# Sixteen GpSimd rectifications of an attention bias, each written as two instructions in two alternating forms

## The chip, the cores and the metric

The kernel runs on one core of a Trainium2 chip. The metric is the device time of one execution in microseconds. TensorE appears in the profile as PE (matmuls) and PEld (weight loads), VectorE as DVE, ScalarE as ACT, GpSimd as POOL and SyncE as SP. All transfers but one are issued by SP.

## The reference, cut to what matters

The input is `q`, `k`, `v` of 8 batches x 8 heads x 576 positions x 64. Attention has a bias that depends on two positions and the head; a gated two-matrix network follows it.

```
rel  = pos[:, None] - pos[None, :]
x    = log1p(|rel|) / log1p(max(pos, 1))[:, None]     # 576 x 576
h    = maximum(x[..., None] * w1 + b1, 0)             # 32 hidden units
bias = h @ w2                                         # one value per head, row, column
out  = softmax(q k^T / 8 + bias) v   -> gated network -> 8 x 576 x 512
```

## The kernel before, in words

**The bias stage.** The first 65 us of the run make the bias, 16 rows of it at a time, in 36 blocks (`bias_rows(m)`, lines 294 to 386). log1p(|rel|) has the same values in every row, so one table `gt` (128 partitions x 576) serves all rows. The 128 partitions hold 4 groups of 32 hidden units, and a *rectification* (`relu`, lines 310 to 325) takes four of the block's rows at once: it multiplies `gt` by a number per partition (`sct`, which holds w1 / log1p(row)), and takes the maximum with another number per partition (`nb1`, which is -b1). So what it stores is max(x w1, -b1) = max(x w1 + b1, 0) - b1, and the constant that is left over is added later through `cadd`. The width is `w`, the longer side of the block's rows, between 304 and 576 columns. A block has four rectifications: the first is always on ScalarE (line 316, a true relu), the other three on VectorE or GpSimd (line 318). Of these 108, 92 are on VectorE and 16 on GpSimd.

Then TensorE multiplies the four results by `w28` (line 337, 4 matmuls to one bank of PSUM, or 8 to two banks), ScalarE and VectorE copy the result out forward and mirrored (lines 356 and 358), and SP stores it to DRAM (line 383), from where it is read back as rows of the bias (line 406).

**What sets the order.** Nothing is decided at run time. `ORDER` is a packed table that gives the sequence of all tasks and the engine of each; every engine works through its own list in that sequence, and semaphores hold an instruction until what it reads has been written and what it overwrites has been read. The results of rectifications lie in three sets of four buffers (`rel=3` in `BUFS`). So a rectification waits until TensorE has read the block of three before, and a block's matmuls wait for its four rectifications. In the same 65 us the first attention scores (line 702, line 748) and the preparation of the weights of the gated network (lines 420 to 444, on VectorE) are put between the blocks.

**After the bias.** The rest of the run computes scores (line 702), adds the bias and finds row maxima on VectorE (line 748), takes exponentials on ScalarE (line 760), normalizes, transposes, multiplies by `v` (line 958) and runs the gated network (lines 1219, 1285). GpSimd has other work there, such as the products of line 810 (scores times 1/sum, 128 x 576) and the differences of line 218. Almost every one-input product that GpSimd makes has the form of `copy` and `scalars` (lines 199, 202): multiply, then multiply again, the second time by 1.0.

Of the kernel before, what the change touches and what calls it, by code (L numbers as in the profile page):

```python
# [18 lines left out]
ALU = mybir.AluOpType  # L19
# [83 lines left out]
class Plan:  # L103
# [3 lines left out]
    def add(self, engines, fn, deps=(), pri=0.0, takes=(), uses=(), hold=0.5):  # L107
        t = Task(engines, fn, [d for d in deps if d is not None], takes)
        t.at = self.at
        for b in uses:  # L110
            b.users.append(t)
        self.tasks.append(t)
        return t
# [25 lines left out]
def attention_gated_mlp(  # L139
# [18 lines left out]
    V, A, G, T, SP = nc.vector, nc.scalar, nc.gpsimd, nc.tensor, nc.sync  # L158
# [14 lines left out]
    def new(b, shape, dt):  # L173
        n = int(np.prod(shape[1:])) // (2 if dt == F16 else 1)
        if b.ring not in SLOT:
            b.t = pools[b.ring].tile(shape, dt, name="t_" + b.ring, tag=f"{b.ring}{b.slot}")
            return b.t
        if (b.ring, b.slot) not in standing:
            standing[b.ring, b.slot] = pools[b.ring].tile([P, SLOT[b.ring]], F32, name=f"t_{b.ring}{b.slot}")
        t = standing[b.ring, b.slot][:, 0:n]  # L180
        if dt != F32:
            t = t.bitcast(dt)
        if len(shape) == 3:
            t = t.rearrange("p (a b) -> p a b", a=shape[1])
        elif len(shape) == 4:
            t = t.rearrange("p (a b c) -> p a b c", a=shape[1], b=shape[2])
        b.t = t
        return t

    def bank(b):  # L190
        return new(b, [P, 512], F32)
# [66 lines left out]
    b1t = bp.tile([P, 1], F32, name="b1t")  # L258
# [8 lines left out]
    sct = bp.tile([P, S // 4], F32, name="sct")  # L267
# [3 lines left out]
    nb1 = bp.tile([P, 1], F32, name="nb1")  # L271
# [19 lines left out]

    stored = {}

    def bias_rows(m):


        plan.at = ("bias", m)
        c = 16 * m // P
        pri = 2 * c - 6 + (m % 8) * 0.25
        i0 = 16 * m  # L300
        wf, wb = S - i0, i0 + 16
        w = max(wf, wb)
        cuts = (0, w) if w <= 512 else (0, w // 2, w)
        pieces = list(zip(cuts, cuts[1:]))
        rel = [Buf("rel") for _ in range(4)]
        pbs = [Buf("tt") for _ in pieces]
        be = Buf("be")
        rts = []

        def relu(e, g):  # L310
            mm = 4 * m + g
            src = gt[:, 0:w]
            if g == 0:
                for x in range(4):
                    rel[x].t = bp.tile([P, S], F32, name="rel", tag=f"rel{x}_{rel[0].slot}")
                A.activation(out=rel[g].t[:, 0:w], in_=src, func=AF.Relu, bias=b1t, scale=sct[:, mm : mm + 1])
            else:
                (G if e == "G" else V).tensor_scalar(  # L318
                    out=rel[g].t[:, 0:w],
                    in0=src,  # L320
                    scalar1=sct[:, mm : mm + 1],
                    scalar2=nb1,
                    op0=ALU.mult,
                    op1=ALU.max,
                )

        for g in range(4):
            eng = [("A", 0.22 + 0.54 * w / S)] if g == 0 else [("V", 0.15 + 0.35 * w / S), ("G", 1.2 + 1.2 * w / S)]
            rts.append(
                add(eng, partial(relu, g=g), rts[:1], pri, [rel[0]] if g == 0 else ())  # L330
            )

        def bias_mm(e, j):
            pb = bank(pbs[j])
            x, y = pieces[j]
            for g in range(4):
                T.matmul(  # L337
                    pb[32 * g : 32 * g + 32, 0 : y - x],
                    lhsT=w28,
                    rhs=rel[g].t[:, x:y],  # L340
                    start=True,
                    stop=True,
                    tile_position=(0, 32 * g),
                )

        def bias_fin(e, j, lo, hi, back):
            if j == 0 and not back:
                new(be, [P, S + 16], F32)
            x = pieces[j][0]
            i = pbs[j].t[:, lo - x : hi - x]  # L350
            if back:
                o = be.t[:, wb - hi : wb - lo][:, ::-1]
            else:
                o = be.t[:, wb - 1 + lo : wb - 1 + hi]
            if e == "A":
                A.activation(out=o, in_=i, func=AF.Identity, bias=cadd)  # L356
            else:
                V.tensor_scalar(out=o, in0=i, scalar1=cadd, scalar2=None, op0=ALU.add)

        fs, bs = [], []  # L360
        first = None
        for j, (x, y) in enumerate(pieces):
            t = add([("P", 0.2 + 0.52 * (y - x) / HS)], partial(bias_mm, j=j), rts, pri + 0.3, [pbs[j]], [rel[0]])
            for back, n, l in ((False, wf, fs), (True, wb, bs)):
                lo, hi = max(x, 1 if back else 0), min(y, n)
                if lo >= hi:
                    continue
                f = add(
                    [("A", 0.2 + 0.19 * (hi - lo) / 288), ("V", 0.1 + 0.31 * (hi - lo) / 288)],
                    partial(bias_fin, j=j, lo=lo, hi=hi, back=back),  # L370
                    [t, first, consts],
                    pri + 0.5,
                    [be] if first is None else (),
                    [pbs[j]],
                )
                first = first or f
                l.append(f)

        def bias_store(e):
            r = i0 - c * P  # L380
            d = bias_f[c][r * ROW : (r + 16) * ROW].rearrange("(o x) -> o x", x=ROW)[:, 0 : H * PITCH]
            d = d.rearrange("o (h y) -> o h y", y=PITCH)
            SP.dma_start(d[:, :, P - 16 - r : P + S - 1 - r], be.t[:, 0 : S + 15])

        s = add([("S", 0.84)], bias_store, fs + bs, pri + 0.6, (), [be], 0.65)
        stored.setdefault(c, []).append(s)

    for m in range(S // 16):
        bias_rows(m)
# [1068 lines left out]
```

## Time and profile before

| | us |
|---|---|
| median of 3 runs | 663.69 |
| lowest, highest | 659.8, 665.06 |
| the profiled execution | 663.0 |
| its span in the profile | 661.2 |

1.8 us of the profiled execution lie outside the span. The span is what the rows of a trace add up to; the runs of the same kernel differ by 5.3 us among themselves. In the rows, "busy" is time in which an engine had an instruction in work, and the words behind an arrow say what ended the idle time before an instruction.

### The profile page before, as it was taken

How to read it: one execution, taken by the hardware profiler on the slowest of the kernel's cores; microseconds unless marked ns; L12 is line 12 of the kernel's file. 1: busy time of each engine (PE TensorE's matmuls, PEld its weight loads, DVE VectorE, ACT ScalarE, POOL GpSimd, SP SyncE). 2: the span in 40 equal slices, each digit the busy share in tenths (PEclk: the TensorE clock that was granted, in tenths of full speed). 3: DMA queues.
4: the chain of work that ended last, by engine and by line, in shares of the span. 5: the costliest groups of instructions: out<-in, count | busy, mean ns of one | idle time of the engine just before them, and what ended most of it. 6: DMA issues, size and time to landing. Idle time of an engine off the chain costs nothing.

```text
span 661.2 us, 16769 instructions
## 1 busy us (share of the span) xinstructions
PE 626.6 (95%) x6176; PEld 405.1 (61%) x6176; DVE 596.0 (90%) x1604; ACT 573.5 (87%) x1268; POOL 489.2 (74%) x539
## 2 busy tenths in 40 slices
PE   6869999999799999999998999999999999999997
PEld 2213667766466677657665576666676765767663
DVE  7999999999999799899998888998988889989982
ACT  6989999999899999889787999889889878989671
POOL 5576739676699898897788788887868868776430
PEclk9969999999999999999999999999999999999999
DMA  5879966336999999999999999999984998999622
GB/s 178 270 254 326 333 242 182 103 140 145 170 209 190 207 218 211 234 192 216 204 209 234 212 208 206 224 184 208 217 179 120 161 210 178 219 196 162 120 80 95
DMA packets 279106, 129.76 MB, mean 196 GB/s; under 512 B 255600, under 2 KB 255856, under 8 KB 279024
## 3 DMA queue, kind: packets, MB, share of 16 engines
q1 hardware_dynamic: 278880, 128.40, 89.5%
q8 instruction: 48, 0.79, 0.5%
q14 instruction: 34, 0.28, 0.2%
q10 hardware_dynamic: 144, 0.29, 0.1%
HBM read 44.64 MB, written 20.33 MB: 98 GB/s over the span
## 4 chain that ended last, share of the span: by engine, by line
PE 52%; DVE 13%; DMA 13%; POOL 9%; ACT 9%; issue 3%; SPq 1%; DVEq 0%; POOLq 0%; ACTq 0%
PE t_sp L702 12%; DMA t_pt<-t_d 12%; PE t_ps L958 10%; PE t_ps L1285 8%; PE t_ps L1219 7%; POOL t_d L218 6%; PE t_ps L891 5%; DVE t_d L748 4%; PE t_ps L337 4%; ACT t_d L760 3%; ACT t_d L195 2%; PE t_sp L718 2%; DVE rel L318 2%; PE t_ps L1004 1%; PE t_ps L1028 1%
## 5 line engine op out<-in xcount | busy, mean ns | idle before, releaser
L218 POOL TENSOR_TENSOR t_d<-t_d,t_d 128x128 f16<-128x128 f32 (+1 forms) x180 | 244.3, 1376 | 50.9 <-ACT t_d L195 46.5
L760 ACT ACTIVATE t_d<-t_d,nm 128x576 f32<-128x576 f32 x288 | 221.5, 771 | 24.3 <-DVE nm L748 23.6
L748 DVE CUSTOM_DVE_ANT_0 t_d<-t_sp,bias 128x576 f32<-128x576 f32 x256 | 186.4, 750 | 22.8 <-PE t_sp L702 16.4
L702 PE MATMUL t_sp<-t_qk 64*128 64x288 f32 x1024 | 170.0, 431 | 4.8 <-DVE nm L748 3.7
L958 PE MATMUL t_ps<-t_pt,t_w 128*64 128x256 f16 (+1 forms) x1664 | 122.6, 296 | 7.3 <-DMA t_pt<-t_d 4.1
L702 PEld LDWEIGHTS t_sp<-t_qk 64*128 64x128 f32 x1024 | 96.1, 187 | 52.6 <-DVE nm L748 16.2
L195 ACT CAST t_d<-t_d 128x576 f16<-128x576 f32 x155 | 99.6, 666 | 12.2 <-DMA t_pt<-t_d 7.6
L1219 PEld LDWEIGHTS <-wv 128*128 128x128 f16 x768 | 72.6, 98 | 29.6 <-issue 10.3
L958 PEld LDWEIGHTS <-t_w 128*64 128x64 f16 x1344 | 70.3, 110 | 24.6 <-issue 15.6
L1219 PE MATMUL t_ps<-xh,wv 128*128 128x256 f16 (+1 forms) x480 | 68.3, 286 | 0.0
L1151 DVE SCALAR_TENSOR_TENSOR t_ps<-t_xp,convw,t_ps 128x288 f32<-128x288 f32 x126 | 64.5, 516 | 1.6 <-ACT t_ps L1142 0.4
L1285 PE MATMUL t_ps<-wo,gh 128*128 128x512 f16 x240 | 57.8, 380 | 0.0
L760 ACT ACTIVATION_READ_ACCUMULATOR t_d<-t_d,nm 128x1 f32 x288 | 54.9, 191 | 0.0
L337 PE MATMUL t_ps<-rel,w 128*32 128x280 f32 (+17 forms) x352 | 44.5, 555 | 9.6 <-ACT t_be L356 4.4
L318 POOL TENSOR_SCALAR rel<-gt,sct,nb 128x560 f32<-128x560 f32 (+11 forms) x16 | 37.4, 2341 | 18.1 <-PE t_ps L337 17.8
L810 POOL TENSOR_SCALAR t_d<-t_d,rinv 128x576 f32<-128x576 f32 x56 | 41.9, 761 | 8.6 <-DVE rinv L790 7.6
L318 DVE TENSOR_SCALAR rel<-gt,sct,nb 128x576 f32<-128x576 f32 (+17 forms) x92 | 46.9, 570 | 1.2 <-PE t_ps L337 1.0
L891 PE MATMUL t_ps<-ident,t_d 128*128 128x128 f32 x324 | 43.4, 278 | 1.9 <-POOL t_d L810 0.8
L891 PEld LDWEIGHTS t_ps<-ident,t_d 128*128 128x128 f32 x324 | 35.3, 140 | 14.1 <-issue 4.4
L199 POOL TENSOR_SCALAR t_d<-t_d 128x576 f16<-128x576 f32 x47 | 34.0, 727 | 12.8 <-ACT t_d L760 10.5
L1285 PEld LDWEIGHTS <-gh 128*128 128x128 f16 x240 | 22.3, 99 | 27.4 <-issue 6.0
L195 ACT COPY t_pt<-t_ps 128x512 f32<-128x512 f32 (+1 forms) x82 | 36.2, 489 | 3.2 <-PE t_ps L891 2.8
(149 smaller groups left out, 1081.8 us busy)
## 6 DMA issues: line engine op xcount, KB each, us to landing
t_qk<-qkd SPq DMA_DIRECT2D x32, 576.0 KB, 4.7
bias_d<-t_be SPq DMA_DIRECT2D x36, 295.5 KB, 4.2
bias<-bias_d SPq DMA_DIRECT2D x16, 576.0 KB, 7.2
out<-t_w SPq DMA_DIRECT2D x32, 256.0 KB, 2.6
t_w<-vd SPq DMA_DIRECT2D x24, 320.0 KB, 3.7
t_w<-vn SPq DMA_DIRECT2D x8, 320.0 KB, 4.4
t_d<-wvd SPq DMA_DIRECT2D x4, 512.0 KB, 4.9
t_d<-wod SPq DMA_DIRECT2D x4, 512.0 KB, 4.1
```

The costliest lines, as they stand in the source:

```text
L195: A.copy(out=out, in_=in_)
L218: (V if e == "V" else G).tensor_tensor(out=out, in0=in0, in1=in1, op=ALU.subtract)
L318: (G if e == "G" else V).tensor_scalar(out=rel[g].t[:, 0:w], in0=src, scalar1=sct[:, mm : mm + 1], scalar2=nb1, op0=ALU.mult, op1=ALU.max,)
L337: T.matmul(pb[32 * g : 32 * g + 32, 0 : y - x], lhsT=w28, rhs=rel[g].t[:, x:y], start=True, stop=True, tile_position=(0, 32 * g),)
L702: T.matmul(ts[a][:, j, 0:hw], lhsT=qk.t[r, c * P : (c + 1) * P], rhs=qk.t[r, x : x + hw], start=True, stop=True,)
L748: V.tensor_tensor_reduce(out=part(c, a).rearrange("p (j f) -> p j f", j=2), in0=sp.t[:, :, 0 : S // 2], in1=bias.rearrange("p (j f) -> p j ...
L760: A.activation(out=part(c, a), in_=part(c, a), func=AF.Exp, bias=nms[c][:, a : a + 1], scale=-1.0, accum_out=sums[c][:, a, 0:1],)
L891: T.transpose(t[:, k * P : (k + 1) * P], es[c].t[:, (k0 + k) * P : (k0 + k + 1) * P], ident)
L958: T.matmul(po.t[r, 0:256], lhsT=vt.t[:, v, r], rhs=pt[:, x, :, :] if tr else pt[:, :, x, :], start=(t == 0 and m == 0), stop=(t == 4 and m ...
L1151: V.scalar_tensor_tensor(out=o, in0=x, scalar=wt, in1=t, op0=ALU.mult, op1=ALU.add)
L1219: T.matmul(pm.t[:, 0:w], lhsT=weights["wv"][wi][:, k, d * P : (d + 1) * P], rhs=xb.t[xi][:, k, 0:w], start=(q == 0 and k == 0), stop=(q == ...
L1285: T.matmul(pm.t, lhsT=gb.t[gi][:, k, o : o + P] if o < 256 else gx.t[gi][:, k, :], rhs=weights["wo"][wi][:, k, :], start=(q == 0 and k == ...
```

## The change

GpSimd's rectification is written in two instructions in place of one, and the sixteen take turns between two forms. With `src` the table, `sc` the number per partition and `nb1` = -b1:

- form A (the 1st, 3rd, ... 15th): `src * sc + b1`, then `max(., 0) + nb1`, in place
- form B (the 2nd, 4th, ... 16th): `src * sc * 1.0`, then `max(., nb1)` alone, in place

Both store the same values as before up to rounding. VectorE's and ScalarE's rectifications stay as they are.

```
-        def relu(e, g):
+        def relu(e, g, turns=turns):
...
-                (G if e == "G" else V).tensor_scalar(
-                    out=rel[g].t[:, 0:w],
-                    in0=src,
-                    scalar1=sct[:, mm : mm + 1],
-                    scalar2=nb1,
-                    op0=ALU.mult,
-                    op1=ALU.max,
-                )
+                o, sc = rel[g].t[:, 0:w], sct[:, mm : mm + 1]
+                if e == "V":
+                    V.tensor_scalar(out=o, in0=src, scalar1=sc, scalar2=nb1, op0=ALU.mult, op1=ALU.max)
+                elif turns[0] % 2:
+                    G.tensor_scalar(out=o, in0=src, scalar1=sc, scalar2=1.0, op0=ALU.mult, op1=ALU.mult)
+                    G.tensor_scalar(out=o, in0=o, scalar1=nb1, scalar2=None, op0=ALU.max)
+                else:
+                    G.tensor_scalar(out=o, in0=src, scalar1=sc, scalar2=b1t, op0=ALU.mult, op1=ALU.add)
+                    G.tensor_scalar(out=o, in0=o, scalar1=0.0, scalar2=nb1, op0=ALU.max, op1=ALU.add)
+                turns[0] += e == "G"
```

On GpSimd's list the sixteen rectifications stand in a row, with no other work between them. These are twelve of them before (`rel` is the buffer that is written, `gt` the table, `PE_49` and the like the semaphores of the engines).

```order
L318 TENSOR_SCALAR rel<-gt,sct,nb_133 128x560 [waits DMAHW0_49,DVE_49]
L318 TENSOR_SCALAR rel<-gt,sct,nb_133 128x560
L318 TENSOR_SCALAR rel<-gt,sct,nb_133 128x432 [waits DVE_49,PE_49]
L318 TENSOR_SCALAR rel<-gt,sct,nb_133 128x464 [waits DVE_49,PE_49]
L318 TENSOR_SCALAR rel<-gt,sct,nb_133 128x336 [waits PE_49]
L318 TENSOR_SCALAR rel<-gt,sct,nb_133 128x384 [waits DVE_49,PE_49]
L318 TENSOR_SCALAR rel<-gt,sct,nb_133 128x336 [waits PE_49]
L318 TENSOR_SCALAR rel<-gt,sct,nb_133 128x416 [waits PE_49]
L318 TENSOR_SCALAR rel<-gt,sct,nb_133 128x384 [waits DVE_49,PE_49]
L318 TENSOR_SCALAR rel<-gt,sct,nb_133 128x432 [waits PE_49]
L318 TENSOR_SCALAR rel<-gt,sct,nb_133 128x400 [waits PE_49]
L318 TENSOR_SCALAR rel<-gt,sct,nb_133 128x480 [waits PE_49]
```

The other four are 544, 576, 528 and 512 wide; the mean of the sixteen is 459 columns. The same place in the changed kernel begins so, and goes on in the same pattern.

```order
L327 TENSOR_SCALAR rel<-gt,sct,b1t 128x560 [waits DMAHW3_49,DMAHW0_49,DVE_49]
L328 TENSOR_SCALAR rel<-rel,nb_133 128x560 [waits DVE_49,Pool_49]
L324 TENSOR_SCALAR rel<-gt,sct 128x560
L325 TENSOR_SCALAR rel<-rel,nb_133 128x560 [waits Pool_49]
L327 TENSOR_SCALAR rel<-gt,sct,b1t 128x432 [waits DVE_49,PE_49]
L328 TENSOR_SCALAR rel<-rel,nb_133 128x432 [waits Pool_49]
L324 TENSOR_SCALAR rel<-gt,sct 128x464 [waits DVE_49,PE_49]
L325 TENSOR_SCALAR rel<-rel,nb_133 128x464 [waits Pool_49]
```

Sixteen instructions are added, and each second instruction of a pair waits for GpSimd's own semaphore, that is, for the end of the first. The lists of TensorE, VectorE, ScalarE and SP are the same as before, with the same waits.

## Rows read from the trace of the kernel before

**Rows 1.** The page: the span, and each engine's busy time, share, instructions.

```profile
span 661.2 us, 16769 instructions
PE 626.6 (95%) x6176; PEld 405.1 (61%) x6176; DVE 596.0 (90%) x1604; ACT 573.5 (87%) x1268; POOL 489.2 (74%) x539
```

**Rows 2.** Busy time by stretch (us, number of instructions), granted clock, DMA share, GB/s.

```profile
5.48:60.95 55.47, 46.49 (x354) 15.85 (x354) 53.84 (x125) 48.68 (x100) 37.41 (x17) 0.88 0.81 267
38.90:60.95 22.05, 18.91 (x146) 6.13 (x138) 21.27 (x45) 20.43 (x41) 17.78 (x8) 0.78 0.85 279
```

**Rows 3.** Chain of waits, 5 to 61 us: shares by engine and line.

```profile
by line: PE t_ps L337 42.2%; DVE rel L318 18.5%; ACT rel L316 11.5%; ACT t_be L356 8.5%; PE t_sp L702 8.0%; issue 4.9%; DVE t_be L358 3.8%; DVE t_d L748 2.4%; DVE t_w L423 0.6%; ACT t_d L760 0.4%; DVE convw L469 0.2%; DVEq L358 0.1%; DVE nm
```

**Rows 4.** Waits, 4 to 65 us: who for whom, us, times, longest.

```profile
POOL rel L318 <- PE t_ps L337: 17.8, 9, 3.4
...
PE t_ps L337 <- ACT t_be L356: 4.4, 5, 2.0
...
PE t_ps L337 <- DVE t_be L358: 3.6, 3, 2.3
...
PEld t_ps L337 <- POOL rel L318: 1.6, 2, 1.4
...
PE t_ps L337 <- POOL rel L318: 0.6, 1, 0.6
```

**Rows 5.** Timeline of GpSimd: start, us, what, count [idle before and its releaser].

```profile
5.48 5.21 POOL L318 TENSOR_SCALAR rel<-gt,sct,nb 128x560 f32<-128x560 f32 x2
14.12 2.64 POOL L318 TENSOR_SCALAR rel<-gt,sct,nb 128x432 f32<-128x432 f32 x1 [3.42 <-PE t_ps L337]
19.15 2.64 POOL L318 TENSOR_SCALAR rel<-gt,sct,nb 128x464 f32<-128x464 f32 x1 [2.39 <-PE t_ps L337]
...
45.11 6.84 POOL L318 TENSOR_SCALAR rel<-gt,sct,nb 128x400 f32<-128x400 f32 x3 [1.51 <-PE t_ps L337]
53.22 4.74 POOL L318 TENSOR_SCALAR rel<-gt,sct,nb 128x576 f32<-128x576 f32 x2 [1.26 <-PE t_ps L337]
58.63 2.33 POOL L318 TENSOR_SCALAR rel<-gt,sct,nb 128x512 f32<-128x512 f32 x1 [0.67 <-PE t_ps L337]
```

**Rows 6.** GpSimd's groups by shape, whole run: busy us, mean ns of one.

```profile
L810 POOL TENSOR_SCALAR t_d<-t_d,rinv 128x576 f32<-128x576 f32 x56 | 41.9, 761 | 8.6 <-DVE rinv L790 7.6 <-DVE bsc L582 1.0
...
L318 POOL TENSOR_SCALAR rel<-gt,sct,nb 128x576 f32<-128x576 f32 x1 | 2.5, 2501 | 1.3 <-PE t_ps L337 1.3
...
L202 POOL TENSOR_SCALAR gtmp<-t_xp,bsc 128x256 f32<-128x256 f32 x4 | 1.9, 481 | 0.3
...
L202 POOL TENSOR_SCALAR bsc<-bsc 128x1 f32<-128x1 f32 x5 | 1.2, 244 | 1.7 <-DVE bsc L576 1.4
```

**Rows 7.** Timeline at 443 us, GpSimd and below it VectorE.

```profile
443.45 1.86 POOL L1113 TENSOR_SCALAR t_w<-t_xp,convw 128x576 f32<-128x576 f32 x1
...
443.38 1.41 DVE L218 TENSOR_TENSOR t_d<-t_d,t_d 128x1024 f16<-128x1024 f32 x2
```

**Rows 8.** Timeline of VectorE at 53 us.

```profile
53.27 0.33 DVE L358 TENSOR_SCALAR t_be<-t_ps,cadd 128x112 f32<-128x112 f32 x1 [0.32 <-ACT t_be L356]
53.52 0.75 DVE L748 CUSTOM_DVE_ANT_0 t_d<-t_sp,bias 128x576 f32<-128x576 f32 x1
```

**Rows 9.** VectorE's rectifications, 10.7-14.1 and 14.12-16.8 us: min/median/max ns.

```profile
L318 DVE TENSOR_SCALAR rel<-gt,sct,nb x5: 527/530/537, 11.2 to 13.7; 128x496 f32<-128x496 f32 x3, 128x512 f32<-128x512 f32 x2
...
L318 DVE TENSOR_SCALAR rel<-gt,sct,nb x6: 537/546/773, 13.7 to 16.3; 128x528 f32<-128x528 f32 x3, 128x512 f32<-128x512 f32 x2, 128x432 f32<-128x432 f32 x1
```

**Rows 10.** Timeline of GpSimd at 74 us: a product, and one that waits for it.

```profile
74.52 0.69 POOL L208 TENSOR_SCALAR t_w<-t_w,wrow 128x512 f32<-128x512 f32 x1
75.30 1.16 POOL L209 TENSOR_TENSOR t_w<-t_w,wo 128x512 f32<-128x512 f32 x1
```

**Rows 11.** Timeline of TensorE's weight loads, 10 to 24 us.

```profile
10.96 0.82 PEld L337 LDWEIGHTS t_ps<-rel,w 128*32 128x32 f32 x12 [0.26 <-POOL rel L318]
...
21.84 0.15 PEld L337 LDWEIGHTS t_ps<-rel,w 128*32 128x32 f32 x6 [1.38 <-POOL rel L318]
```

More of the change, by code (lines that the diff above doesn't have):

```diff
@@ L292, in attention_gated_mlp @@
     stored = {}
+    turns = [0]
     def bias_rows(m):
```

## The prediction

> **What bounds the kernel now.** I read the page first, then the stretch of the sixteen rectifications by busy time, its chain of waits, its waits, and last GpSimd's instructions one by one. The page says that the run is TensorE's: busy 626.6 of 661.2 us [rows 1]. A delay of the bias stage in front is therefore not made up later; I carry it to the end one for one. The stretch from the first rectification on GpSimd to the end of the last, 5.48 to 60.95 us, is another matter: there VectorE is the fullest, 53.84 of 55.47 us, TensorE has 46.49 and GpSimd 37.41 [rows 2]. The chain of waits through it runs over TensorE's line 337, VectorE's and ScalarE's rectifications and their copies; among the shares that the row shows, none is GpSimd's [rows 3]. GpSimd is idle 17.8 us there, always because TensorE has not yet freed a buffer, and TensorE waits for GpSimd in three places, 1.6 + 0.6 = 2.2 us [rows 4]. So there is little to gain: with rectifications that cost GpSimd nothing, 2.2 us or 0.3% could come back. And there are 18.1 us of room (55.47 - 37.41) before GpSimd is the bound.
>
> **What one rectification costs now.** 37.41 us over sixteen is 2.34 us each [rows 2], at a mean width of 459. A multiply-multiply product of GpSimd takes 0.761 us at 576 columns and 0.481 us at 256 [rows 6], 0.875 ns per column on 0.257 us; at 459 columns that is 0.66 us. Two things can make up the difference of 1.7 us, and the change depends on which.
>
> The first is the form. The one that starts at 53.22 us is 576 wide and takes 2.5 us [rows 5, 6]. For its first microsecond VectorE works on a copy out of PSUM and on line 748 [rows 8], beside which line 810 keeps its 0.75 us in most of its 56 cases (mean 0.761) [rows 6]. A product of 0.76 us would have been over in that microsecond; this was not. So multiply-then-maximum with two numbers per partition is itself dearer than multiply-multiply.
>
> The second is the neighbour. While GpSimd is idle VectorE's rectifications of 496 and 512 columns take 527 to 537 ns; while one of GpSimd's runs, the longest of the next six takes 773 [rows 9]. They get in each other's way, and GpSimd more: a multiply-multiply of 576 columns that falls on two back-to-back two-input operations of VectorE takes 1.86 us instead of 0.76 [rows 7]. One rectification lengthens about two of VectorE's by 0.23 us each, with ordinary ones between (773 against 537 is the row that I can show); I read that as two separate claims on the memory, as if the instruction went over its data twice.
>
> [...]
>
> **The change part by part.** VectorE, ScalarE, TensorE and SP keep their lists and waits; the order shows sixteen more instructions on GpSimd and nothing else.
>
> *The wait inside a pair.* The second instruction starts when the first has finished. A product that ends at 75.21 us is followed by one that waits for it at 75.30 [rows 10]: 0.1 us per pair.
>
> *An instruction that goes over its data once.* No row has it beside VectorE's rectifications. Its ends are 0.66 us, the bare price, and 0.66 + (1.86 - 0.76) = 1.76 us, with the longest hold-up shown [rows 6, 7]. VectorE is at 97%, so some hold-up is the rule; two claims in 2.34 us suggest about 1.2 each. I take 1.35.
>
> *Form B* is the multiply-multiply of line 810 and then a maximum alone. For a maximum alone there is no wide row; the nearest is a maximum with a multiply on one column, 0.244 us [rows 6], no more than the 0.257 that a product starts with. I take both at 1.35: 1.35 + 0.1 + 1.35 = 2.8, 0.46 more than now. Ends: 1.4 (both bare) and 1.35 + 0.1 + 2.34 = 3.8 (the second as dear as today's form).
>
> *Form A* begins with two numbers per partition and two different operations, as today's instruction does, so its nearest row is the 2.34. The second has one number per partition; I take one pass in a full stretch, 1.6, between 1.35 and 1.76. 2.34 + 0.1 + 1.6 = 4.04, 1.7 more than now. Ends: 1.4 and 2.34 + 0.1 + 2.34 = 4.8.
>
> *GpSimd's sum.* 8 x 1.7 + 8 x 0.46 = 17.3 us more: 54.7 of 55.5. It just fits on the whole, but not in each place. In front, an A and a B come back to back, end at 10.69 us, and TensorE takes them at 10.96 [rows 5, 11]: 2.2 us later less 0.3 is 1.9 us late. At 21.84 TensorE takes a B the moment it ends [rows 11]: 0.46 late. From 38.90 on, eight rectifications fill 17.78 of 22.05 us [rows 2], room 4.3; four A and four B add 4 x 1.7 + 4 x 0.46 = 8.6, so 4.3 us too much. The rest lie in gaps of 2 to 3.4 us [rows 5] and are covered. Together 6.7 us late. TensorE's matmuls wait 4.4 + 3.6 us for ScalarE and VectorE in the same stretch [rows 4], and these two can run ahead while GpSimd is late; I let half be swallowed: **+3.4**. Ends 0 and 6.7.
>
> *VectorE's share.* Eight A with one claim more, 8 x 0.23 = 1.8 us on the fullest engine; part of it falls where TensorE is late anyway: **+1.1**.
>
> Sum: 663.0, the profiled execution's time, + 3.4 + 1.1 = **667.5 us**. That execution stands 0.7 us under the median of 663.69, so this is +0.6% against the median. What a measurement of this kernel can tell from no change is about 1%, 6.6 us.
>
> **The rivals.**
>
> *Level: every new instruction goes once.* If multiply-add with two numbers is as cheap as multiply-multiply, a pair costs 1.4 to 2.8 us, the sum of claims on VectorE stays, and GpSimd's lateness stays inside its gaps. For: the bare price of line 810. Time 660.8 (the 2.2 us of waits gone) to 664, most likely 663. Chance 0.27.
>
> *Slower: GpSimd becomes the bound of the stage.* All of A's and B's second cost what today's form costs; multiply-multiply alone is cheap. For: nearly every one-input GpSimd instruction of this kernel multiplies twice, so no other form has a wide row that is cheap; the only other one is the 2.34. Against: the maximum on one column costs nothing extra. Then A is 4.8, B 3.8, sixteen take 69 us against a stretch of 55.5: 13 us late, and 24 more claims on VectorE, 5.5 us, partly beside it: 676 to 681. With B's maximum cheap it is 8 x 4.8 + 8 x 2.8 = 61 us, 5.5 over plus the uneven places, 671 to 675. It decides as soon as the sixteen together pass 55 us. TensorE's granted clock is 0.78 of full from 38.9 to 60.95 us already [rows 2], and more waiting would not raise it. Together chance 0.37, middle 676. [...]
>
> *Faster by more than 1%.* It would need VectorE to win 7 us, all that GpSimd takes from it now (16 x 2 x 0.23). No row speaks for that. 0.03.
>
> **How the numbers follow.** The forecast, 664 to 670, has 0.33. Within 1% (657.1 to 670.3) lie the level case and nearly all of the forecast: 0.27 + 0.31 = 0.58. Slower by over 1%: 0.37 + 0.02 = 0.39. Faster 0.03. The range goes from 661, the low end of the level case, to 680, near the top of the slower one; left out are the gain, the lowest part of the level case and the last of the slow one, under 0.2.
>
> **What would show it.** By GpSimd's groups: line 324 near 1.35 us, 327 near 2.3, 325 near 1.35, 328 near 1.6. GpSimd's busy time in the stage near 55 us, its idle time for freed buffers nearly gone, TensorE's wait for GpSimd up from 2.2 to 6 us or so, the last matmul of line 337 some 4 us later. Wrong if 327 is as short as 324 (then level), or if 325 and 328 take over 2 us (then slower, and GpSimd takes a large share of the chain of waits).

## The result, and the profile after

The changed kernel takes 666.61 us in the median of 20 runs (663.9 to 669.43), the kernel before, on the same chips, 662.61 us in the median of 20 (658.77 to 665.08). The ratio is 1.0065, 95% interval 1.005 to 1.0081: 4.0 us slower, where the forecast was 667.5 us and +0.6%. The profiled execution took 668.65 us, its span is 666.9.

The page of the changed kernel, the line that answers to [rows 1]:

```profile
PE 629.1 (94%) x6176; PEld 406.9 (61%) x6176; DVE 600.0 (90%) x1604; ACT 572.9 (86%) x1268; POOL 496.1 (74%) x555
```

Busy time by stretch of the changed kernel (us of the stretch, then PE, PEld, DVE, ACT and POOL, the granted clock, DMA share, GB/s). The first stretch answers to the first of [rows 2], from the first rectification on GpSimd to the end of the last; the second reaches from VectorE's first in the stage to where GpSimd goes on after it.

```profile
5.23:63.53 58.30, 46.24 (x354) 15.88 (x354) 57.68 (x125) 49.26 (x101) 44.10 (x33) 0.94 0.81 265
4.50:67.44 62.94, 50.07 (x390) 17.62 (x390) 62.32 (x138) 53.38 (x111) 44.76 (x43) 0.95 0.80 259
```

The same second stretch in the kernel before (the same 390 matmuls and 138 VectorE instructions):

```profile
4.70:64.86 60.16, 50.32 (x390) 17.62 (x390) 58.50 (x138) 53.37 (x111) 38.14 (x26) 0.89 0.82 268
```

The stretch is 2.8 us longer, TensorE works as long as before at a granted clock that is no lower, and **VectorE works 3.8 us longer on the same instructions**. It is busy for 62.32 of 62.94 us. Where its time goes stands in the groups by line. First VectorE's rectifications in the kernel before:

```profile
L318 DVE TENSOR_SCALAR rel<-gt,sct,nb 128x576 f32<-128x576 f32 (+17 forms) x92 | 46.9, 570 | 1.2 <-PE t_ps L337 1.0
```

Then, in the changed kernel, VectorE's and GpSimd's (count, busy us, mean ns of one, idle time before them; VectorE's instructions overlap a little, so its busy time is less than count times mean: 50.4 us against 92 x 0.611 = 56.2):

```profile
L322 DVE TENSOR_SCALAR rel<-gt,sct,nb 128x576 f32<-128x576 f32 (+17 forms) x92 | 50.4, 611 | 0.5 <-PE t_ps L341 0.3
...
L328 POOL TENSOR_SCALAR rel<-rel,nb 128x336 f32<-128x336 f32 (+6 forms) x8 | 14.7, 1835 | 0.9
L325 POOL TENSOR_SCALAR rel<-rel,nb 128x560 f32<-128x560 f32 (+7 forms) x8 | 13.0, 1628 | 0.8
L327 POOL TENSOR_SCALAR rel<-gt,sct,b1t 128x336 f32<-128x336 f32 (+6 forms) x8 | 10.3, 1286 | 10.6 <-PE t_ps L341 10.6
L324 POOL TENSOR_SCALAR rel<-gt,sct 128x560 f32<-128x560 f32 (+7 forms) x8 | 6.2, 780 | 2.0 <-PE t_ps L341 2.0
```

The 92 rectifications that the change does not touch went from 46.9 to 50.4 us: 3.5 of the 3.8. GpSimd's sixteen pairs take 14.7 + 13.0 + 10.3 + 6.2 = 44.2 us and 1.7 us of waiting inside pairs, 8.5 more than the 37.4 of [rows 2].

The chain of waits of the changed kernel, 5 to 66 us, against [rows 3]:

```profile
by line: DVE rel L322 48.9%; POOL rel L328 9.0%; PE t_ps L341 7.8%; POOL rel L325 6.2%; POOL rel L327 5.5%; issue 4.4%; DVE t_be L362 3.6%; POOL rel L324 2.5%; ACT rel L318 1.9%; PE t_sp L706 1.9%; DVE t_w L424 1.8%; DVE t_w L427 1.5%; DVE 
```

Before, line 337's matmuls led with 42.2% and VectorE's rectifications had 18.5%. Now VectorE's have 48.9%, and GpSimd's, which had no share that the row shows, 23.2% in four rows. The waits of the changed kernel, 4 to 72 us, against [rows 4]:

```profile
PEld t_ps L341 <- POOL rel L325: 3.2, 2, 2.1
PEld t_ps L341 <- POOL rel L328: 2.2, 4, 0.9
PE t_ps L341 <- POOL rel L325: 1.9, 2, 1.6
...
PE t_ps L341 <- POOL rel L328: 0.4, 1, 0.4
```

TensorE waits 7.7 us for GpSimd, where it was 2.2. So two things happened, VectorE was slowed and GpSimd is late, and these rows alone do not tell which of them made the 4 us. GpSimd's timeline in the changed kernel, start, us and in brackets the idle time before:

```profile
13.99 1.50 POOL L327 TENSOR_SCALAR rel<-gt,sct,b1t 128x432 f32<-128x432 f32 x1 [2.22 <-PE t_ps L341]
...
53.06 2.11 POOL L328 TENSOR_SCALAR rel<-rel,nb 128x544 f32<-128x544 f32 x1
55.15 0.74 POOL L324 TENSOR_SCALAR rel<-gt,sct 128x576 f32<-128x576 f32 x1
55.99 2.02 POOL L325 TENSOR_SCALAR rel<-rel,nb 128x576 f32<-128x576 f32 x1
58.00 0.91 POOL L327 TENSOR_SCALAR rel<-gt,sct,b1t 128x528 f32<-128x528 f32 x1
59.01 2.12 POOL L328 TENSOR_SCALAR rel<-rel,nb 128x528 f32<-128x528 f32 x1
...
67.60 1.47 POOL L814 TENSOR_SCALAR t_d<-t_d,rinv 128x576 f32<-128x576 f32 x2
```

At 55 us the 0.74 us of a multiply-multiply stand beside the 2.02 of a maximum alone, both 576 wide: the maximum is the dear half. The last row is the first work of GpSimd after the bias stage, at 67.60 us; I use its start as **the end of the stage** below.

### The profile page after: what moved, and what is told of

Read it like the earlier page. It is cut to its first block, busy times and chain, and to the rows that moved or that the text cites. A ratio compares the mean times of both kernels' runs of the same rounds, so it can differ in the third digit from the quotient of the medians.

```text
span 666.9 us, 16784 instructions
## 1 busy us (share of the span) xinstructions
PE 629.1 (94%) x6176; PEld 406.9 (61%) x6176; DVE 600.0 (90%) x1604; ACT 572.9 (86%) x1268; POOL 496.1 (74%) x555
## 4 chain that ended last, share of the span: by engine, by line
PE 50%; DVE 17%; DMA 12%; POOL 8%; ACT 8%; issue 3%; SPq 1%; DVEq 0%; ACTq 0%; POOLq 0%
PE t_sp L706 13%; PE t_ps L962 11%; DMA t_pt<-t_d 9%; PE t_ps L1289 8%; PE t_ps L1223 8%; DVE t_d L752 5%; PE t_ps L895 5%; DVE rel L322 4%; POOL t_d L218 4%; ACT t_d L764 3%; ACT t_d L195 2%; PE t_sp L722 2%; DMA t_qk<-qkd 2%; PE t_ps L1008 1%; PE t_ps L1032 1%
## 5 line engine op out<-in xcount | busy, mean ns | idle before, releaser
L962 PE MATMUL t_ps<-t_pt,t_w 128*64 128x256 f16 (+1 forms) x1664 | 125.3, 300 | 7.9 <-DMA t_pt<-t_d 4.9
L962 PEld LDWEIGHTS <-t_w 128*64 128x64 f16 x1344 | 72.1, 112 | 26.1 <-issue 15.4
L341 PE MATMUL t_ps<-rel,w 128*32 128x288 f32 (+17 forms) x352 | 44.1, 511 | 12.6 <-ACT t_be L360 4.3
L322 DVE TENSOR_SCALAR rel<-gt,sct,nb 128x576 f32<-128x576 f32 (+17 forms) x92 | 50.4, 611 | 0.5 <-PE t_ps L341 0.3
L895 PEld LDWEIGHTS t_ps<-ident,t_d 128*128 128x128 f32 x324 | 35.3, 140 | 14.1 <-issue 4.4
L341 PEld LDWEIGHTS t_ps<-rel,w 128*32 128x32 f32 x352 | 13.9, 113 | 40.9 <-ACT t_be L360 12.3
```

The lines of the kernel that those rows point to most:

```text
L322: V.tensor_scalar(out=o, in0=src, scalar1=sc, scalar2=nb1, op0=ALU.mult, op1=ALU.max)
L341: T.matmul(pb[32 * g : 32 * g + 32, 0 : y - x], lhsT=w28, rhs=rel[g].t[:, x:y], start=True, stop=True, tile_position=(0, 32 * g),)
L895: T.transpose(t[:, k * P : (k + 1) * P], es[c].t[:, (k0 + k) * P : (k0 + k + 1) * P], ident)
L962: T.matmul(po.t[r, 0:256], lhsT=vt.t[:, v, r], rhs=pt[:, x, :, :] if tr else pt[:, :, x, :], start=(t == 0 and m == 0), stop=(t == 4 and m ...
```

## The experiments

Theory 1: VectorE's time. It is full in the stage; every GpSimd instruction lengthens some of VectorE's, and two instructions lengthen more than one. Theory 2: GpSimd's lateness; TensorE waits for its results. All versions in one table. The ratio is to the kernel before in the same comparison, where its median was 663.09 (the four versions from "all in form A" on), 663.6 (all on VectorE) and 662.3 (the last two); VectorE's column is the busy time of its rectifications in the stage, from the traces; the last three columns too are from single traces. The last is the time from 4.70 us, where VectorE's rectifications begin within 0.25 us in every trace, to the end of the stage, less what VectorE is busy in it. VectorE has the same instructions in its list in the first six versions. So a loss from lengthened instructions makes VectorE busier, and a loss from lateness, on an engine that would otherwise be full, has to show as idle time of VectorE.

| version | median us | ratio [95%] | VectorE's rectifications, us | TensorE's waits for GpSimd's rectifications, us | end of the stage | VectorE idle in the stage, us |
|---|---|---|---|---|---|---|
| before (two traces) | 662.61 | 1 | 46.9, 46.3 (92) | 2.2, 5.1 | 65.04, 63.63 | 1.66, 0.84 |
| changed (two traces) | 666.61 | 1.0065 [1.005, 1.0081] | 50.4, 51.3 (92) | 7.7, 5.7 | 67.60, 69.01 | 0.62, 0.92 |
| all in form A | 668.08 | 1.0078 [1.0047, 1.011] | 51.4 (92) | 13.1 | 68.84 | 0.98 |
| all in form B | 667.35 | 1.007 [1.0045, 1.0095] | 50.7 (92) | 4.2 | 67.89 | 0.69 |
| unread products added | 665.85 | 1.0057 [1.0029, 1.0084] | 49.8 (92) | 0.8 | 66.32 | 0.25 |
| small products in front | 665.24 | 1.0055 [1.0027, 1.0083] | 45.4 (92) | 21.1 | 65.92 | 4.09 |
| all on VectorE | 664.21 | 1.002 [0.9992, 1.0047] | 47.1 (108) | 0 | 63.55 | 0.59 |
| the same, GpSimd's unread, old form | 672.07 | 1.0144 [1.0111, 1.0177] | 54.7 (108) | 0 | 71.48 | 0.17 |
| the same, GpSimd's unread, two forms | 677.5 | 1.0222 [1.0186, 1.0258] | 60.3 (108) | 0 | 77.06 | 0.58 |

**A second trace of each.** No edit to either kernel.

> The kernel before, unchanged, for a second trace. The bias stage of the first trace ends where GpSimd's first product of line 810 starts, 65.0 us. If that stage repeats within 0.3 us, the 2.6 us that the change adds there are the change's own, and what the medians differ by beyond them lies in later stages; if it is over 1 us shorter here, the change costs more in the stage than the two traces show.

> The changed kernel, unchanged, for a second trace: the bias stage 2.6 us longer than before if the stage repeats; the 3.1 us that its first trace lost after 160 us should not repeat in the same places if they are chance.

The stage did not repeat within 0.3 us: in the kernel before it ended 1.4 us earlier, in the changed one 1.4 us later than in the first traces. Its end is 64.3 in the mean of the two traces of before and 68.3 in those of the change, 4.0 us apart, as are the medians. The executions took 662.78 and 668.89 us, so each pair of profiles differs by some 6 us where the medians differ by 4.0; single traces are good to about 1.5 us here. The 3.1 us that the first changed trace lost behind the stage did not come back: behind its end the spans have 596.2 and 599.3 us in the first pair, 597.4 and 598.1 in the second.

From 4.70 us to the end of the stage, second traces, before and then changed (the columns as above):

```profile
4.70:63.63 58.93, 47.21 (x390) 17.09 (x390) 58.09 (x138) 53.23 (x111) 38.77 (x27) 0.94 0.82 273
4.70:69.01 64.31, 52.25 (x390) 16.97 (x390) 63.39 (x139) 53.72 (x111) 44.39 (x44) 0.95 0.80 254
```

VectorE is 5.3 us busier here (3.6 in the first pair, from 4.70 us on) and idle for 0.92 us against 0.84 (0.62 against 1.66 in the first pair). What the stage gained in length is busy time of VectorE; idle time, which lateness would have left, did not grow by more than 0.1 us.

**One form at a time.** All sixteen in form A, or all in form B:

```
-                elif turns[0] % 2:
+                elif False:       # the other kernel: elif True:
```

> All sixteen rectifications of GpSimd in form A (multiply-add, then maximum-add). In the changed kernel's profile a pair of A takes 3.22 us with the wait (1.29 + 0.1 + 1.83), a pair of B 2.51 (0.78 + 0.1 + 1.63), before 2.34. Theory 1, VectorE's time: both forms claim the memory three times where the old one claims it twice, so it does not matter which form stands where; all-A costs the same as the change, 0.65% over before (0.4 to 0.9%), and VectorE's 92 rectifications are 50.4 us busy, as in the change. Theory 2, GpSimd's lateness: an A adds 0.88 us, a B 0.17; all-A adds 16 x 0.88 = 14 us to GpSimd's list where the change adds 8.4, so 1.1% or more.

> All sixteen in form B (multiply-multiply, then maximum alone). Theory 1, VectorE's time: the same three claims, so 0.65% over before again (0.4 to 0.9%), VectorE's 92 rectifications again about 50 us. Theory 2, GpSimd's lateness: only 16 x 0.17 = 2.7 us added to GpSimd's list, of which its 17.8 us of idle time swallow nearly all: 0 to 0.2% over before.

GpSimd's rows, all A first, then all B:

```profile
L328 POOL TENSOR_SCALAR rel<-rel,nb 128x560 f32<-128x560 f32 (+11 forms) x16 | 30.6, 1911 | 1.6
L327 POOL TENSOR_SCALAR rel<-gt,sct,b1t 128x560 f32<-128x560 f32 (+11 forms) x16 | 16.4, 1024 | 12.2 <-PE t_ps L341 12.1
```

```profile
L325 POOL TENSOR_SCALAR rel<-rel,nb 128x560 f32<-128x560 f32 (+11 forms) x16 | 25.3, 1579 | 1.5
L324 POOL TENSOR_SCALAR rel<-gt,sct 128x560 f32<-128x560 f32 (+11 forms) x16 | 14.8, 922 | 16.5 <-PE t_ps L341 16.5
```

All in A is 16.4 + 30.6 = 47.0 us for GpSimd, all in B 40.1, only 2.7 more than before. By theory 2 the one should lose clearly and the other hardly at all. They lose the same within their intervals, 0.78 and 0.70%, and VectorE's rectifications are lengthened alike, to 51.4 and 50.7 us. The 0.7 us that A is above B in the median, and 0.95 us in the end of the stage, are as much as lateness could be worth between the two; of the 0.95 us VectorE's idle time has 0.3 (0.98 against 0.69). The intervals do not resolve it.

**Claims without lateness.** The kernel before, with twelve multiply-multiply products on GpSimd that nobody reads, each behind a rectification that is followed by idle time:

```
+                if e == "G":
+                    for _ in range(EXTRA.get(turns[0], 0)):   # {1: 2, 2: 2, 3: 2, 5: 2, 7: 2, 9: 1, 12: 1}
+                        spare = biasr[0][:, 0, 0:w]
+                        G.tensor_scalar(out=spare, in0=src, scalar1=sct[:, mm : mm + 1], scalar2=1.0, op0=ALU.mult, op1=ALU.mult)
+                    turns[0] += 1
```

> The kernel before, with twelve more multiply-multiply products of the table by GpSimd that nobody reads, written to a buffer that is not yet in use, and put behind those rectifications after which GpSimd is idle for over 1.2 us: no rectification ends later because of its own list, but VectorE is claimed against twelve times more. Theory 1, VectorE's time: 12 x 0.22 = 2.6 us on VectorE's rectifications (46.9 to 49.5 us), about three quarters of the change's loss: 0.3 to 0.6% over before. Theory 2, GpSimd's lateness: no change, 0 to 0.1%.

```profile
L320 DVE TENSOR_SCALAR rel<-gt,sct,nb 128x576 f32<-128x576 f32 (+17 forms) x92 | 49.8, 601 | 0.1
L320 POOL TENSOR_SCALAR rel<-gt,sct,nb 128x560 f32<-128x560 f32 (+11 forms) x16 | 35.8, 2238 | 12.0 <-PE t_ps L344 11.6 <-DVE rel L320 0.3
L331 POOL TENSOR_SCALAR biasr<-gt,sct 128x432 f32<-128x432 f32 (+5 forms) x12 | 8.7, 722 | 0.5
```

TensorE waits less for GpSimd than before (0.8 us), and the kernel is 0.57% slower, as theory 1 said; VectorE is idle for no more than 0.25 us of the stage.

**Lateness without claims.** The kernel before, with two products of one column in front of each of the sixteen:

```
+                if e == "G":
+                    for x in range(2):
+                        G.tensor_scalar(out=rel[g].t[:, x : x + 1], in0=gt[:, x : x + 1], scalar1=sct[:, mm : mm + 1], scalar2=1.0, op0=ALU.mult, op1=ALU.mult)
```

> The kernel before, with two products of one column (into the first two columns of the same buffer, overwritten by the rectification) in front of each of GpSimd's sixteen rectifications: each ends later by 0.4 us if the two run at their bare 0.22, up to 1.5 us if they are held up by VectorE; they hardly hold VectorE up themselves. Theory 1, VectorE's time: no change, 0 to 0.15%. Theory 2, GpSimd's lateness: 16 x 0.5 = 8 us added to GpSimd's list, as much as the change adds (8.4): 0.5 to 0.8% over before.

```profile
L321 DVE TENSOR_SCALAR rel<-gt,sct,nb 128x576 f32<-128x576 f32 (+17 forms) x92 | 45.4, 553 | 2.0 <-PE t_ps L340 1.9
...
L320 POOL TENSOR_SCALAR rel<-gt,sct 128x1 f32<-128x1 f32 x32 | 12.9, 417 | 8.8 <-PE t_ps L340 8.7
...
PEld t_ps L340 <- POOL rel L321: 13.1, 10, 3.2
PE t_ps L340 <- POOL rel L321: 8.0, 6, 2.4
```

From 4.70 us to the end of the stage:

```profile
4.70:65.92 61.22, 45.30 (x390) 17.01 (x390) 57.13 (x138) 53.45 (x111) 49.00 (x60) 0.97 0.81 265
```

Here theory 1 missed. VectorE's rectifications got no longer, and the kernel lost 0.55% all the same: 12.9 us of small products on GpSimd's list (11.0 net, because its rectifications went from 37.4 to 35.5), TensorE's waits up to 21.1 us, 2.1 us in the medians and 0.55% or 3.6 us by the ratio. So lateness counts too, at a sixth to a third of what is put on GpSimd's list, and theory 1 alone is not the law of this stage. But this loss looks different in the trace: VectorE is less busy than before, 57.13 us, and idle for 4.09.

**GpSimd taken out.** All sixteen on VectorE:

```
-                (G if e == "G" else V).tensor_scalar(
+                V.tensor_scalar(
```

> The kernel before with GpSimd's sixteen rectifications given to VectorE, at the same places of the order. VectorE's own work grows by sixteen of about 0.43 us (its rectifications of 459 columns follow each other in that time), 6.9 us; GpSimd's 32 claims, which lengthen VectorE's instructions by 0.2 us each, go: 6 to 7 us. Theory 1, VectorE's time: the two cancel, VectorE is as long busy in the bias stage as before, and TensorE's waits for GpSimd (2.2 us) go: 0 to 0.4% faster than before. Theory 2, GpSimd's lateness: VectorE, the fullest engine, gets 6.9 us more and only the 2.2 us of waits go: 0.3 to 0.7% slower than before.

```profile
L318 DVE TENSOR_SCALAR rel<-gt,sct,nb 128x560 f32<-128x560 f32 (+17 forms) x108 | 47.1, 501 | 0.5 <-PE t_ps L337 0.3
```

The time is 0.2% over before, with an interval from -0.1 to +0.5% that holds part of both forecasts and decides nothing; VectorE's row is as theory 1 said. With sixteen more to do, VectorE is as long busy with rectifications, 47.1 us for 108, as before with 92. Undisturbed one costs it 47.1 / 108 = 0.44 us; 92 would be 40.1. So in the kernel before GpSimd's sixteen took 46.9 - 40.1 = 6.8 us from VectorE, 0.42 each, which is what VectorE needs to make them itself. In the changed kernel they take 50.4 - 40.1 = 10.3 us, 0.64 each.

**Both causes apart, at full size.** On top of the last version, GpSimd makes its sixteen as well, into a buffer that is not read; once in the old form, once in the change's two:

```
+                V.tensor_scalar(out=o, in0=src, scalar1=sc, scalar2=nb1, op0=ALU.mult, op1=ALU.max)
+                o = biasr[0][:, 0, 0:w]
                 if e == "V":
-                    V.tensor_scalar(out=o, in0=src, scalar1=sc, scalar2=nb1, op0=ALU.mult, op1=ALU.max)
+                    pass
```

> All 108 rectifications that TensorE reads are on VectorE and ScalarE, as in the version with all on VectorE. In addition GpSimd makes its sixteen in the old single form, into a buffer that nobody reads, so no engine waits for GpSimd. Theory 1 (VectorE's time: each GpSimd instruction lengthens two of VectorE's): 16 x 0.42 to 0.65 us = 6.7 to 10.4 us on VectorE, which is full in this stage, so 1.0 to 1.6% over the version with all on VectorE (ratio about 1.012 to 1.018 to the kernel before); VectorE's rectifications 54 to 57 us. Theory 2 (only GpSimd's lateness counts): nobody waits for it, so the time stays that of the version with all on VectorE, a ratio of 1.002.

> As the other, with GpSimd's unread rectifications in the change's two forms, two instructions each in turns. Theory 1: 16 x 0.29 = 4.6 us more on VectorE than the old form, so 0.6 to 0.7% slower than the other, as much as the change itself cost, though nobody waits for GpSimd; VectorE's rectifications 58 to 62 us. Theory 2: GpSimd's extra time is not waited for, so the same time as the other, within 0.2%.

VectorE's and GpSimd's groups, the old form first:

```profile
L321 DVE TENSOR_SCALAR rel<-gt,sct,nb 128x560 f32<-128x560 f32 (+17 forms) x108 | 54.7, 571 | 0.0
L326 POOL TENSOR_SCALAR biasr<-gt,sct,nb 128x560 f32<-128x560 f32 (+11 forms) x16 | 34.0, 2122 | 1.5
```

```profile
L321 DVE TENSOR_SCALAR rel<-gt,sct,nb 128x560 f32<-128x560 f32 (+17 forms) x108 | 60.3, 623 | 0.4 <-PE t_ps L343 0.3
L330 POOL TENSOR_SCALAR biasr<-biasr,nb 128x336 f32<-128x336 f32 (+6 forms) x8 | 15.0, 1881 | 0.9
L327 POOL TENSOR_SCALAR biasr<-biasr,nb 128x560 f32<-128x560 f32 (+7 forms) x8 | 12.2, 1525 | 0.8
L329 POOL TENSOR_SCALAR biasr<-gt,sct,b1t 128x336 f32<-128x336 f32 (+6 forms) x8 | 6.5, 813 | 0.7
L326 POOL TENSOR_SCALAR biasr<-gt,sct 128x560 f32<-128x560 f32 (+7 forms) x8 | 5.6, 703 | 0.8
```

In neither trace does TensorE wait for a rectification of GpSimd. The two forms still cost 677.5 - 672.07 = 5.4 us more than the one, and VectorE's rectifications 60.3 - 54.7 = 5.6 us more. That is 0.8%, a little over theory 1's 0.6 to 0.7, where theory 2 had nothing. The old form, unread, costs 7.9 us over the version without by the medians, which are of two comparisons, and 8.2 us by the ratios (7.6 us of VectorE's). So a microsecond taken from VectorE in this stage is a microsecond of the run, and **the split into two instructions takes at least the change's 4.0 us from VectorE with nobody late**. So VectorE's time is enough to make the whole loss: the change's 4.0 us have the size of what its rectifications gained in the two pairs of traces (3.5 and 5.0 us). Of a share of lateness the traces show nothing: VectorE has no more idle time in the changed kernel than before (0.62 and 0.92 us against 1.66 and 0.84), where the version that is only late has 4.09. By the loss per microsecond of list in that version 1.4 to 2.8 us of lateness would have been possible (a sixth to a third of 8.5); what lateness there was fell where VectorE was busy anyway. Single traces leave up to about a microsecond of it open.

**The price of each form.** A program of its own that leaves the kernel's computation out: GpSimd runs fourteen forms of the instruction, four of each (two of 576 columns, two of 288), first with VectorE idle, then beside VectorE's rectifications of 512 columns without a gap.

```
+    run(lambda o, w: G.tensor_scalar(out=o, in0=gt[:, 0:w], scalar1=s1, scalar2=s2, op0=ALU.mult, op1=ALU.add))
+    run(lambda o, w: G.tensor_scalar(out=o, in0=gt[:, 0:w], scalar1=s1, scalar2=None, op0=ALU.mult))
...
+    for n in range(500):
+        V.tensor_scalar(out=ring[n % 4], in0=gt[:, 0:512], scalar1=s1, scalar2=s2, op0=ALU.mult, op1=ALU.max)
```

> Another program, which measures GpSimd's forms by themselves and leaves the computation out: fourteen forms of its one-input instruction, 576 and 288 columns, each twice; first with VectorE idle, then beside a stream of VectorE rectifications of 512 columns. If the maximum is what is dear: multiply-multiply, multiply-add (one or two numbers per partition) and their single forms 0.75 to 0.95 us at 576 with VectorE idle, every form with a maximum or minimum 1.2 to 1.6 us. If two numbers per partition are dear: multiply-multiply and multiply-add with two such numbers 1.2 us or more, a maximum alone 0.75. If a second, different operation is dear: every mixed pair 1.2 or more, single operations 0.75. Beside VectorE: forms of 0.75 rise to 1 to 1.5 us, the dear ones to 2 to 2.5 with two lengthened VectorE instructions each.

With VectorE idle, 576 columns (mean ns of one). Line 46 is multiply and subtract, 39 multiply and maximum (the old form), 40 maximum and add (A's second), 37 one multiply, 41 one maximum (B's second), 34 multiply and multiply by 1.0 (B's first; the program's first instruction is one of these two), 36 multiply and add (A's first), 35 two multiplies by two numbers per partition:

```profile
L46 POOL TENSOR_SCALAR alone<-gt,s,s 128x576 f32<-128x576 f32 x2 | 4.6, 2288 | 0.0
L39 POOL TENSOR_SCALAR alone<-gt,s,s 128x576 f32<-128x576 f32 x2 | 4.5, 2277 | 0.0
L40 POOL TENSOR_SCALAR alone<-gt,s 128x576 f32<-128x576 f32 x2 | 4.4, 2207 | 0.0
...
L37 POOL TENSOR_SCALAR alone<-gt,s 128x576 f32<-128x576 f32 x2 | 3.4, 1718 | 0.0
L41 POOL TENSOR_SCALAR alone<-gt,s 128x576 f32<-128x576 f32 x2 | 3.4, 1712 | 0.0
...
L34 POOL TENSOR_SCALAR alone<-gt,s 128x576 f32<-128x576 f32 x2 | 1.8, 880 | 3.4 <-DMA gt<-grel 3.4
L36 POOL TENSOR_SCALAR alone<-gt,s,s 128x576 f32<-128x576 f32 x2 | 1.6, 818 | 0.0
L35 POOL TENSOR_SCALAR alone<-gt,s,s 128x576 f32<-128x576 f32 x2 | 1.6, 810 | 0.0
```

None of the three cases of the expectation came out: one operation alone is dear, a multiply as much as a maximum (1.72 and 1.71 us), a pair of multiplies or adds is cheap (0.81 to 0.88 us), and a pair with a maximum or a subtraction is the dearest (2.21 to 2.29 in these rows). What in the instruction makes these prices is not shown.

And VectorE's stream beside one of line 39, which runs from 105.67 us for 2.67 us. The first row is GpSimd's, two in a row; the others are three of the four rectifications of VectorE that start in the first of them:

```profile
105.67 5.34 POOL L39 TENSOR_SCALAR beside<-gt,s,s 128x576 f32<-128x576 f32 x2
...
105.88 1.04 DVE L57 TENSOR_SCALAR ring<-gt,s,s 128x512 f32<-128x512 f32 x1
107.29 0.54 DVE L57 TENSOR_SCALAR ring<-gt,s,s 128x512 f32<-128x512 f32 x1
107.75 0.88 DVE L57 TENSOR_SCALAR ring<-gt,s,s 128x512 f32<-128x512 f32 x1
```

Alone, VectorE starts one every 0.456 us (219 in 100 us). The old form lengthens one at its beginning (1.04 us) and one at its end (0.88), those between take the ordinary 0.54: by the starts it costs VectorE 0.50 + 0.34 = 0.84 us at 576 columns and 0.36 at 288. Maximum and add costs 0.76 and 0.28, a maximum alone the same, multiply and add one lengthened rectification of 1.04 us, 0.51 and 0.27, multiply and multiply by 1.0 costs 0.43 and 0.19. Between these, at 459 columns, the old form takes 0.65 us from VectorE, form A 0.41 + 0.57 = 0.98, form B 0.33 + 0.57 = 0.90: 0.29 more, 16 x 0.29 = 4.6 us for the change if VectorE had no other work. The stage, where it has some, shows 3.5 and 5.0, the unread pair 5.6.

## Why the prediction was right, and by which errors

- **The total** (+0.6%, 667.5 us) came out, its split did not. The forecast was 3.4 us of lateness and 1.1 us of VectorE's time; by the traces it is VectorE's time: its rectifications take 3.5 and 5.0 us more, and it is idle no longer than before. Two terms were wrong in opposite directions, and their sum was near by luck.
- **The bound** held: VectorE is the fullest in the stage, and what the stage loses is carried to the end, 4.0 and 4.0 us. I read this off [rows 2] and then priced GpSimd's lists instead of VectorE's.
- **VectorE's share** failed in count and size. I counted one claim more for A only, eight at 0.23 us. B also takes more from VectorE than the old form: at 576 columns in the micro program its multiply costs 0.43 us and its maximum 0.76, the old form, which lengthens two rectifications, 0.84. And a claim is not 0.23 us: the row of 773 against 537 ns [rows 9] was one of a range, and the micro program has 0.34 to 0.51 at 576 columns. Sixteen at about 0.29 net are 4.6 us. Charging every GpSimd instruction its lengthened neighbours, A and B alike, would have given the total for the right reason.
- **GpSimd's sum** failed: 17.3 us forecast, 8.5 measured. A's first instruction was priced at 2.34 us after today's form, because both have two numbers per partition and two operations. It takes 1.29 us in the mean and 0.91 in a row, and the micro program shows that neither property costs anything (810 and 818 ns). B's first was 0.78, not 1.35. The second instructions were 1.83 (forecast 1.6) and 1.63 (forecast 1.35), for another reason than the hold-up that I put there: at 576 columns, undisturbed, a lone maximum takes 1.71 us and maximum and add 2.21. The wait inside a pair was 0.1 us, as read.
- **Two passes over the data**, as a reading of [rows 9], priced the parts wrongly. By it a lone maximum should have gone over its data once and cost what multiply-multiply costs. It does not: a lone maximum or a lone multiply takes 1.7 us with VectorE idle, and beside VectorE a lone maximum costs it 0.76 us, nearly the old form's 0.84. The old form takes 2.28 us at 576 columns with VectorE idle and 2.67 beside it, so the hold-up is some 0.4 us. What the instruction does inside is not shown.
- **Lateness**: TensorE's waits for GpSimd were forecast at 6 us and measured at 7.7 and 5.7, but the second trace of before has 5.1 of them already, and a wait is not a loss where VectorE ends last anyway. All in B has 4.2 us of them and loses as much as all in A with 13.1.
- **The level rival** got its mark, line 327 is nearly as short as 324 (0.91 and 0.74 in a row), but not its result, because it kept the sum of claims. **The slow rival** had the dear maximum right in part (2.0 to 2.1 us at 528 to 576 columns in a row) and GpSimd as the bound wrong: it is busy for 44.10 of 58.30 us. One of its signs came all the same, GpSimd's share of the chain of waits, 23.2% and in the second trace 33.0%; the sign did not tell the two cases apart. That more waiting would not raise TensorE's granted clock is not what the rows show: from 38.90 to 60.95 us its mean is 0.78 of full speed in the first trace of before and 0.85 in the first changed one; over the stage it is 0.89 and 0.94 in the two traces of before, 0.95 in both changed ones, and 0.97 in the version with small products, where TensorE waits 21.1 us for GpSimd. What sets the clock is not shown.
- **Two lengthened and ordinary ones between**, as read off [rows 9], came out for the old form: in the micro program VectorE runs at its usual 0.54 us in the middle of a GpSimd instruction of 2.67 us and loses 0.84 of it.
- **The maximum as the dear operation** does not explain the prices: one multiply alone takes 1.718 us and one maximum 1.712, and multiply and subtract 2.288 where multiply and maximum takes 2.277.

Left open: the experiments' medians stand 0.5 to 2.6 us further from before than the ends of their stages do (all in B 4.3 us by the medians of its comparison, 3.6 by the stage; the unread old form 9.8 and 7.1). Behind the end of the stage the spans have 595.4 to 599.3 us in the eleven traces, 596.2 and 597.4 of them before, so with one trace each I can't say whether that is a loss behind the stage or the spread of single executions. None of the versions beat the kernel before.

## What to carry to other kernels

Price work on GpSimd by what it takes from a full VectorE beside it: count the lengthened VectorE instructions per GpSimd instruction, and compare with VectorE doing the work itself, which here cost the same 0.42 to 0.44 us. Splitting one GpSimd instruction into two added to VectorE's time here even where nobody waited for GpSimd: 5.6 us in the unread pair. The chain of waits does not settle which of the two engines costs the time: it gave VectorE's rectifications 48.9% and GpSimd's 23.2%. The full engine's own time did, split into busy and idle: here lengthened neighbours made it busier (62.32 us against 58.50), lateness made it idle (4.09 us). Before a form is priced by a row that resembles it, measure the form by itself: here the operation pair decided (0.81 us for two multiplies, 2.28 for multiply and maximum, each by two numbers per partition), and the operands hardly did (2.13 us for multiply and maximum by two constants).

## What the runs showed of the hardware

- GpSimd's `tensor_scalar` on 576 columns of f32 has three prices with VectorE idle: a pair of multiplies or adds 0.81 to 0.88 us (0.88 with the program's first instruction in the mean), one operation of any kind tried 1.64 to 1.72, a pair with a maximum or a subtraction 2.13 to 2.29. One multiply (1.72) costs over twice what a multiply by each of two numbers costs (0.81).
- GpSimd and VectorE disturb each other at the ends of an instruction: in the program of forms multiply and add lengthens one VectorE rectification (1.04 us, where 0.54 is usual), the old form two, at its beginning and its end (1.04 and 0.88). By the starts, at 576 columns, that is 0.51 and 0.84 us of VectorE's time.
- The first GpSimd instruction after an idle time took much longer in some cases. A multiply-multiply of 512 columns that starts into a full VectorE stream took 1.82 us; the next two, of 576 columns and without a gap, took 0.82 in the mean. In the changed kernel line 327 took 0.95 to 2.03 us after idle, at 336 to 432 columns, and 0.91 in a row at 528 and 544. It is no rule: with all in B, a multiply-multiply of 512 columns took 0.69 us after 0.72 us of idle. What decides it is not shown.
